# Earlier weight loads, tables inside the pipeline and a new order of steps in a fused linear-attention and soft-MoE kernel

## The chip, the cores and the metric

The kernel runs on one core of one Trainium2 chip. The metric is the device time of one execution in microseconds (us); lower is better. Three runs of the kernel before gave a median of 171.94 us.

## The reference, cut to what matters

A recurrent linear attention over S = 768 tokens for 4 batches and 8 heads of width 48 feeds a soft mixture of experts. The program computes both in one launch.

```python
for t in range(S):                       # per batch b and head h
    cur = einsum('bhd,bhe->bhde', u*k_t, v_t)
    y[:,:,t] = einsum('bhd,bhde->bhe', r_t, state + cur)
    state = w[:,:,None]*state + einsum('bhd,bhe->bhde', k_t, v_t)
x = y as (3072, 384)
logits = x @ phi                          # phi (384, 32): 8 experts x 4 slots
slot_input = softmax(logits, 0).T @ x
for e in range(8):
    slot_out[e] = relu(slot_input[e] @ w1[e]) @ w2[e]    # w1 (384,1024), w2 (1024,384)
out = softmax(logits, 1) @ slot_out
```

## The kernel before, in words

**Work units.** Heads are taken in pairs: pair m = 4b+q is heads 2q and 2q+1 of batch b, so there are 16 pairs. Each pair has two halves of 384 tokens, which gives 32 half-pairs; the main loop (L423) runs steps i = -5 to 31, and step i finishes half-pair i. The decay is applied by tables: `table(0,q)` for k and `table(1,q)` for r are a product on VectorE (L161) and an exponential on ScalarE (L163), made from `w_rep`, the vector w copied to all partitions (loaded at L95, its logarithm at L156). All eight tables are written ahead of the loop.

**Data.** `raw` has two buffers; batch b uses buffer b % 2, with a k, an r and a v part. `load_batch` issues three transfers on SyncE's queue (k and r in L103, v in L107): k and r move in 1024 runs of 1152 bytes each, v in 2048 runs of 576 bytes. Batches 0 and 1 are asked for at the start; batch 2 is asked for in the code of step 2 and batch 3 in that of step 10, each part as soon as GpSimd or ScalarE has read the old contents. In this text k(2), r(2), v(2) are the three parts of batch 2.

**One pair's way through the engines.** `scale(m,0)` and `scale(m,1)` on GpSimd multiply k and r by their tables into `kr`, which has three buffers (L201). TensorE transposes six tiles of k into bank T0 and six of r into T1 (`t_pe`, L208); ScalarE copies them out as kT and rT (L214). TensorE turns kT back into rows in bank T0 (`b_pe`, L220), and VectorE copies those out as `kn` (L225, the row copy). VectorE multiplies T1 with kT into `prod` (L230, the product). For half-pair i: `v_cast` on ScalarE turns a batch half of v into bf16 (L239, once for 8 steps' worth of two halves), `v_pe` and `v_evac` (L254, L260) lay v out, `a_pe` (L269) makes the score tiles in the one bank pair Ab, VectorE masks them (`mask_f`, L274), `m_pe` (L284 to L299) makes the states in bank Mb, VectorE reads those (`z_evac`, L309 to L315: Z0, Z and dv), `y_pe` (L325 to L338) adds up the output and `y_evac` (L345) copies it to x. `route` (L402) does the softmax part of half-batch n over four steps; in every fourth step from step 12 on it also runs `disp` (L391), which writes bank Mb, and its read on VectorE (L396, L398).

**Order.** Every engine runs its instructions in the order of the code. In a step the transposes into T0 or T1 come first, then a, the mask, the product and row copy (both in odd steps), v, y, m, Z and dv, then `route`.

**Weights.** `load_w(n)` is issued by GpSimd behind the `scale` of its step, n = 0 to 7 for w1 (L121) and 8 to 15 for w2 (L124); called w0 to w15 here. They are turned to bf16 on the way. w1 moves in 384 runs of 4 KB a load (2 KB written), w2 in 128 runs of 12 KB (6 KB written). `W_AT` says at which step how many are issued, from step 3 on. The four last w2 loads go into buffer 0 of `raw`.

**The tail.** After the loop the last softmax parts run, then for each expert 24 small matmuls whose stationary operand is a slice of w1 with every 8th column (L512, `fo:F:nF`), then 24 with contiguous slices of w2 (L527), then the output (L547 to L553).

Of the kernel before, what the change touches and what calls it, by code (L numbers as in the profile page):

```python
# [9 lines left out]
def kernel(  # L10
# [41 lines left out]
    def O(ins):  # L52
        return tc.keep_in_program_order(ins)
# [37 lines left out]

    w_rep = cst.tile([128, H * D], f32, name="w_rep")
    wu = cst.tile([8, 128], f32, name="wu")
    O(dve.memset(wu[:], 1.0))
    O(act.dma_start(out=w_rep[:], in_=w.flatten().partition_broadcast(128)))  # L95
    wu3 = wu[:].rearrange("q (e s) -> q e s", s=64)
    O(act.dma_start(out=wu3[0:4, :, 0:D], in_=w.rearrange("(q e) d -> q e d", e=2)))
    O(act.dma_start(out=wu3[4:8, :, 0:D], in_=u.rearrange("(q e) d -> q e d", e=2)))
    O(act.preload_act_table_set("natural_log_exp_and_others"))
    phi_f = cst.tile([128, nM, ES], f32, name="phi_f")  # L100

    def load_kr(which, src, b):
        O(sp.dma_start(out=raw_of(which, b).rearrange("p (h x) -> p h x", h=H),  # L103
# [6 lines left out]
    def load_batch(b):  # L110
        load_kr(0, k, b)
        load_kr(1, r, b)
        load_v(b)

    load_batch(0)
    O(sp.dma_start(out=phi_f[:], in_=moe_phi.rearrange("(mo p) s -> p mo s", p=128)))
    load_batch(1)

    def load_w(n):
        if n < E:  # L120
            O(pool.dma_start(out=w1_all[:, n, :, :],  # L121
                             in_=moe_w1[n].rearrange("(mo p) f -> p mo f", p=128)))
        else:
            O(pool.dma_start(out=w2_of(n - E),  # L124
                             in_=moe_w2[n - E].rearrange("(p fo) d -> p fo d", p=128)))


    s_i = cst.tile([128, J], i32, name="s_i")
# [38 lines left out]
    for j in range(1, NKR):
        O(dve.memset(kr_t[j][:], 0.0))
    table(0, 1)
    table(1, 1)  # L170
# [8 lines left out]
    O(pe.transpose(Yb[:, 0:8], wu[:], ident_f[0:8, 0:8]))  # L179
    wuT = cst.tile([128, 8], f32, name="wuT")  # L180
    O(dve.tensor_copy(wuT[:], Yb[:, 0:8]))
    O(dve.tensor_mul(ucol[0:64, :, 0], wuT[0:64, 0:4], wuT[0:64, 4:8]))
    O(dve.tensor_mul(ucol[64:128, :, 1], wuT[64:128, 0:4], wuT[64:128, 4:8]))
    wT = cst.tile([128, nQ], f32, name="wT")
    O(act.activation(out=wT[:], in_=wuT[:, 0:4], func=AF.Ln))
    O(act.activation(out=wT[:], in_=wT[:], func=AF.Exp, scale=float(T)))
    for q in range(2, nQ):
        table(0, q)
        table(1, q)

# [195 lines left out]
    def disp(n, first):  # L386
        x, Le = st["x", n], st["Le", n]
        for mi in range(nM + 1):
            for c in range(L):
                lhs = x[:, c, mi * C:(mi + 1) * C] if mi < nM else ones[:]  # L390
                O(pe.matmul(ds_p[:, mi * ES:(mi + 1) * ES], lhs, Le[:, c, :],  # L391
                            start=(first and mi == 0 and c == 0), stop=(c == L - 1), skip_group_check=True))

    def disp_ev(n):
        if n == 0:
            O(dve.tensor_copy(acc[:], ds_p))  # L396
        else:
            O(dve.tensor_add(acc[:], acc[:], ds_p))  # L398

    LAG = 2 * nQ  # L400

    def route(i):  # L402
        n, s = divmod(i - LAG, nQ)
        if s == 0 and 0 <= n - 1 < nG:
            disp(n - 1, False)
            disp_ev(n - 1)
            le_t(n - 1)
        if 0 <= n < nG:
            if 1 <= s <= L:
                lg_mm(n, s - 1)  # L410
            if s < L:
                xt_mm(n, s)
        if s == 0 and 0 <= n - 1 < nG:
            let_ev(n - 1)
        if 0 <= n < nG:
            if s == L:
                le_ev(n)
            if s < L:
                xt_ev(n, s)

    W_AT = {3: 1, 5: 1, 7: 1, 9: 1, 11: 1, 13: 1, 15: 1, 17: 1, 19: 1, 20: 1, 21: 1, 22: 1, 23: 4}
    nw = 0
    for i in range(-5, nH):  # L423
        m2, odd = divmod(i, 2)
        mk = m2 + 2
        if odd == 0:
            if 0 <= mk < nU:
                t_pe(mk, 0)
                t_evac(mk, 0)
        elif 0 <= mk < nU:  # L430
            t_pe(mk, 1)
            t_evac(mk, 1)
            b_pe(mk)
        if odd == 1:
            if 0 <= m2 + 3 < nU:
                scale(m2 + 3, 0)
        elif 0 <= m2 + 2 < nU:
            scale(m2 + 2, 1)
        if i % 8 == 4 or i % 8 == 5:
# [3 lines left out]
        if 0 <= i + 1 < nH:
            a_pe(i + 1)
            mask_f(i + 1)
        if odd == 1 and 0 <= mk < nU:
            prod_f(mk)
            b_evac(mk)
        if 0 <= i + 2 < nH:
            v_pe(i + 2)  # L450
            v_evac(i + 2)
        if 0 <= i < nH:
            y_pe(i)
            y_evac(i)
        if 0 <= i + 1 < nH:
            m_pe(i + 1)
            z_evac(i + 1)
# [126 lines left out]
```

## Time and profile before

| | |
|---|---|
| median of 3 runs (lowest, highest) | 171.94 us (171.04, 172.51) |
| profiled execution, whole time | 171.09 us |
| its span in the profile | 169.3 us |
| busy TensorE, VectorE, ScalarE, GpSimd | 66%, 63%, 51%, 35% of the span |
| granted TensorE clock, mean of the span | 0.872 |

A profile row gives start and duration in us. A chain row is one piece of the chain of work that ended last. "L201" is a line of the kernel. In a row of instructions "[1.70 <-DMA ...]" is the idle time of the engine ahead of it and what ended it. PEclk is the granted TensorE clock in tenths, for 40 slices of 4.23 us each.

### The profile page before, as it was taken

The numbers are of one execution on the slowest core, as the hardware profiler recorded it, in microseconds if no ns is written. First come the engines' busy times: TensorE is split into PE (matmuls) and PEld (weight loads), VectorE is DVE, ScalarE is ACT, GpSimd is POOL, SyncE is SP. The second block draws the span as 40 slices with busy tenths as digits, with TensorE's granted clock in tenths as the row PEclk, the third lists the DMA queues.
The fourth block names the chain that finished last, engine by engine and source line by source line (L and its number), as shares of the span: only waits on it lengthen the run. The fifth ranks groups of instructions, "written<-read, shape, count | busy, mean of one in ns | idle before, by whom it ended". The sixth has DMA issues, their size and how long they took to land.

```text
span 169.3 us, 4612 instructions
## 1 busy us (share of the span) xinstructions
PE 112.3 (66%) x1964; PEld 94.1 (56%) x1964; DVE 105.8 (63%) x204; ACT 86.0 (51%) x173; POOL 58.5 (35%) x59
## 2 busy tenths in 40 slices
PE   0021019776877977877876886885976999986750
PEld 0011018665756866666665675674755999972310
DVE  4099921999779889589589589589463000126550
ACT  2142594554566776886576885663454111004560
POOL 5039697666537854656668300000000000000000
PEclk9999999999699999999999999999599655555555
DMA  4999999999999999999999999200000000002896
GB/s 103 288 374 285 390 305 344 326 242 218 233 275 267 283 236 239 233 237 208 210 215 213 225 208 215 49 4 0 6 0 4 0 4 0 4 4 93 348 415 258
DMA packets 22524, 32.00 MB, mean 189 GB/s; under 512 B 1000, under 2 KB 17512, under 8 KB 22504
## 3 DMA queue, kind: packets, MB, share of 16 engines
q0 software_dynamic: 4352, 12.58, 37.9%
q1 hardware_dynamic: 17984, 18.92, 34.1%
q10 hardware_dynamic: 168, 0.20, 0.7%
q8 instruction: 15, 0.25, 0.6%
q14 instruction: 5, 0.04, 0.1%
HBM read 39.57 MB, written 4.72 MB: 262 GB/s over the span
## 4 chain that ended last, share of the span: by engine, by line
PE 48%; DVE 30%; issue 8%; ACT 7%; DMA 4%; DVEq 0%; ACTq 0%
DVE AT L274 9%; PE T L208 8%; DVE kn L225 5%; PE Ab L269 5%; DVE W L161 5%; PE Vb L254 5%; DMA w_rep<-in_w_dram 4%; DVE prod L230 4%; PE Ab L512 4%; PE T L220 3%; PE Mb L391 2%; PE Ab L547 2%; PE Vb L512 2%; PE Xb L512 2%; PE Ab L527 2%
## 5 line engine op out<-in xcount | busy, mean ns | idle before, releaser
L201 POOL TENSOR_TENSOR kr<-raw,W 128x576 bf16<-128x576 f32 x32 | 45.8, 1439 | 37.2 <-PE T L208 18.7
L274 DVE TENSOR_TENSOR AT<-Ab,mask_ut 128x768 bf16<-128x768 f32 x32 | 30.6, 957 | 13.6 <-PE Ab L269 13.5
L208 PE MATMUL T<-ident,kr 128*128 128x128 bf16 x192 | 17.5, 233 | 23.4 <-DVE kn L225 18.6
L208 PEld LDWEIGHTS <-kr 128*128 128x128 bf16 x192 | 13.6, 104 | 25.2 <-issue 20.0
L214 ACT COPY kT<-T 128x768 bf16<-128x768 bf16 x16 | 12.8, 797 | 19.4 <-PE T L208 19.4
L254 PE MATMUL Vb<-v_bf,Q 128*128 128x96 bf16 x288 | 19.2, 216 | 0.0
L230 DVE TENSOR_TENSOR prod<-T,kT 128x768 bf16<-128x768 bf16 x16 | 15.2, 948 | 3.2 <-ACT rT L214 3.2
L254 PEld LDWEIGHTS <-Q 128*128 128x128 bf16 x288 | 14.4, 103 | 3.5 <-issue 0.6
L260 ACT CAST vn<-Vb 128x288 bf16<-128x288 f32 x32 | 12.7, 398 | 5.1 <-PE Vb L254 2.7
L315 DVE TENSOR_TENSOR dv<-vn,Mb 128x288 bf16<-128x288 bf16 x32 | 14.2, 445 | 0.0
L345 ACT CAST x<-Yb 128x288 bf16<-128x288 f32 x32 | 12.8, 399 | 2.3 <-PE Yb L338 2.3
L220 PE MATMUL T<-ident,kT 128*128 128x128 bf16 x96 | 9.0, 237 | 7.1 <-ACT kT L214 7.1
L214 ACT COPY rT<-T 128x768 bf16<-128x768 bf16 x16 | 12.8, 798 | 1.3 <-PE T L208 1.3
L313 DVE TENSOR_TENSOR Z<-Mb,bmask 128x192 bf16<-128x192 f32 x32 | 11.3, 352 | 2.8 <-PE Mb L299 0.9
L512 PEld LDWEIGHTS <-w_all 128*128 128x128 bf16 x192 | 11.9, 168 | 1.3 <-issue 1.2
L295 PE MATMUL Mb<-vn,kn 128*128 128x96 bf16 (+2 forms) x80 | 11.9, 250 | 0.0
L269 PE MATMUL Ab<-rT,kT 64*128 64x128 bf16 x192 | 11.4, 228 | 0.0
L220 PEld LDWEIGHTS <-kT 128*128 128x128 bf16 x96 | 6.8, 107 | 7.4 <-ACT kT L214 7.4
L325 PE MATMUL Yb<-vn,AT 128*128 128x48 bf16 x192 | 10.3, 186 | 0.1
L338 PE MATMUL Yb<-dv,ident 128*128 128x288 bf16 x32 | 9.4, 295 | 0.2
L369 ACT COPY xT<-Xb 128x384 bf16<-128x384 bf16 x18 | 8.5, 473 | 1.9 <-PE Xb L360 1.1
L336 PE MATMUL Yb<-Z,rT 128*128 128x96 bf16 x80 | 8.8, 208 | 0.7 <-DVE Z L313 0.7
(120 smaller groups left out, 215.9 us busy)
## 6 DMA issues: line engine op xcount, KB each, us to landing
w_all<-in_moe_w_dram POOLq DMA_DIRECT2D x8, 768.0 KB, 10.3
raw<-in_k_dram SPq DMA_DIRECT2D x4, 1152.0 KB, 9.1
raw<-in_r_dram SPq DMA_DIRECT2D x4, 1152.0 KB, 11.7
raw<-in_v_dram SPq DMA_DIRECT2D x4, 1152.0 KB, 19.1
w_own<-in_moe_w_dram POOLq DMA_DIRECT2D x4, 768.0 KB, 9.2
raw<-in_moe_w_dram POOLq DMA_DIRECT2D x4, 768.0 KB, 14.5
out_dram<-raw SPq DMA_DIRECT2D x3, 768.0 KB, 3.3
out_dram<-W SPq DMA_DIRECT2D x2, 768.0 KB, 3.6
```

What stands on the lines that cost most here:

```text
L201: O(pool.tensor_mul(kr[:, j].rearrange("p j (h s) -> p j h s", s=64)[:, :, :, 0:D], src, W[j][:, q].rearrange("p j (h d) -> p j h d", h=2)))
L208: O(pe.transpose(bank[:, x * C:(x + 1) * C], kr[:, j, x, :], ident[:]))
L214: O(act.copy(t[:].rearrange("p (s j) -> p s j", j=J), bank[:, 0:S].rearrange("p (j s) -> p s j", j=J)))
L220: O(pe.transpose(T0[:, c * C:(c + 1) * C], kT[:, c * C:(c + 1) * C], ident[:]))
L230: O(dve.tensor_mul(pr[:].rearrange("p (s j) -> p s j", j=J), T1[:, 0:S].rearrange("p (j s) -> p s j", j=J), st["kT", m][:].rearrange("p (s ...
L254: O(pe.matmul(Vb[:, c * P2:(c + 1) * P2], Q3[:, o:o + C], vb[:, 2 * q:2 * q + 2, j, :], start=(j == 0), stop=(j == JV - 1)))
L260: O(act.copy(vn[:].rearrange("p c e d -> p (c e d)"), Vb[:, 0:L * P2]))
L269: O(pe.matmul(Ab[:, e, c * C:(c + 1) * C], kT[s, t], rT[s, t]))
L274: O(dve.tensor_mul(AT[:], Ab[:, :, 0:T].rearrange("p e (c t) -> p e c t", c=L), mask_ut[:, None, None, :].to_broadcast([128, 2, L, C])))
L315: O(dve.tensor_mul(dv[:], st["v", i][:].rearrange("p c e d -> p (c e) d"), Mb[:, 288:288 + 2 * L, None].to_broadcast([128, L * 2, D])))
L345: O(act.copy(st["x", n][:, :, q * P2:(q + 1) * P2], Yb[:, 0:L * P2].rearrange("p (c e) -> p c e", c=L)))
L512: O(pe.matmul(hp[:, fo, :], w1_all[:, e, mi, fo:F:nF], uns[:, mi, e * Spe:(e + 1) * Spe], start=(mi == 0), stop=(mi == nM - 1)))
```

## The change

Line numbers of the changed kernel are a few lower than those of the kernel before from L94 on (L201 becomes L196, L512 becomes L507).

- **Start.** `w_rep` is the first transfer of SyncE's queue instead of the first of ScalarE's; phi comes behind batch 1. Only the padding columns of `kr` are cleared, not the whole tiles. Two small products (`ucol`) go from VectorE to GpSimd, ahead of its first `scale`.
- **Tables.** Only the tables of q = 0 are made ahead of the loop; the other six are made in steps -4 to 1, at the end of a step's code.
- **Order of a step.** a, mask, [even step: product], y, v, m, Z and dv, `scale`, TensorE's part of `route`, then the transposes into T0 or T1, [odd step: rows back and the row copy], `v_cast`, ScalarE's part of `route`, table.
- **Weights.** `W_AT` starts at step -1 instead of 3 and ends at 22 instead of 23. w1 is read in 12 KB runs (128 runs, 6 KB written, three rows of w1 to a partition), w2 in 6 KB runs (256 runs). For that, dispatch takes every third column of x, and L512 takes every 4th column of w1 instead of every 8th.

```diff
-    O(act.dma_start(out=w_rep[:], in_=w.flatten().partition_broadcast(128)))
+    O(sp.dma_start(out=w_rep[:], in_=w.flatten().partition_broadcast(128)))
...
-                             in_=moe_w1[n].rearrange("(mo p) f -> p mo f", p=128)))
+                             in_=moe_w1[n].rearrange("(p mo) f -> p mo f", p=128)))
...
-                             in_=moe_w2[n - E].rearrange("(p fo) d -> p fo d", p=128)))
+            O(pool.dma_start(out=w2_of(n - E).rearrange("p (a y) d -> p a (y d)", y=FB),
+                             in_=moe_w2[n - E].rearrange("(a p y) d -> p a (y d)", p=128, y=FB)))
...
-    O(dve.memset(kr_t[0][:], 0.0))
+    for t in kr_t:
+        O(dve.memset(t[:].rearrange("p a j (e s) -> p (a j e) s", s=64)[:, :, D:64], 0.0))
...
-    for q in range(2, nQ):
-        table(0, q)
-        table(1, q)
...
-                lhs = x[:, c, mi * C:(mi + 1) * C] if mi < nM else ones[:]
+                lhs = x[:, c, mi:Dm:nM] if mi < nM else ones[:]
...
-    W_AT = {3: 1, 5: 1, 7: 1, 9: 1, 11: 1, 13: 1, 15: 1, 17: 1, 19: 1, 20: 1, 21: 1, 22: 1, 23: 4}
+    W_AT = {-1: 1, 1: 1, 3: 1, 5: 1, 7: 1, 9: 1, 11: 1, 13: 1, 15: 1, 17: 1, 19: 1, 20: 1, 21: 2, 22: 2}
...
+        q, j = divmod(i + 6, 2)
+        if 1 <= q < nQ:
+            table(j, q)
...
-                O(pe.matmul(hp[:, fo, :], w1_all[:, e, mi, fo:F:nF],
+                O(pe.matmul(hp[:, fo, :], w1_all[:, e, mi, (fo // FB) * C * FB + fo % FB:(fo // FB + 1) * C * FB:FB],
```

GpSimd of the kernel before, from the scale of pair 3 on (kr0, kr1, kr2 are the three buffers, raw0 and raw1 the two batches, W0 and W1 the k and r tables):

```order
L201 TENSOR_TENSOR kr0_115<-raw0_67,W0_122 128x12x48
L201 TENSOR_TENSOR kr0_115<-raw0_67,W1_123 128x12x48
L201 TENSOR_TENSOR kr1_116<-raw1_68,W0_122 128x12x48
L121 DMA w1_all_69<-in_moe_w1_dram 128x3x1024
L201 TENSOR_TENSOR kr1_116<-raw1_68,W1_123 128x12x48
L201 TENSOR_TENSOR kr2_117<-raw1_68,W0_122 128x12x48
L121 DMA w1_all_69<-in_moe_w1_dram 128x3x1024
```

GpSimd of the changed kernel, from the scale of pair 2 on:

```order
L196 TENSOR_TENSOR kr2_117<-raw0_67,W0_124 128x12x48
L123 DMA w1_all_69<-in_moe_w1_dram 128x3072
L196 TENSOR_TENSOR kr2_117<-raw0_67,W1_125 128x12x48
L196 TENSOR_TENSOR kr0_115<-raw0_67,W0_124 128x12x48
L123 DMA w1_all_69<-in_moe_w1_dram 128x3072
L196 TENSOR_TENSOR kr0_115<-raw0_67,W1_125 128x12x48
L196 TENSOR_TENSOR kr1_116<-raw1_68,W0_124 128x12x48
L123 DMA w1_all_69<-in_moe_w1_dram 128x3072
```

Load w0 now follows the first scale of pair 2 instead of that of pair 4, so each load wn follows pair n+2 instead of n+4; three loads are issued before the second scale of pair 4, and two of them before batch 0's buffer is free for batch 2.

ScalarE of the changed kernel ahead of and in steps -4 and -3 (before, all eight L163 rows stood ahead of the first copy of kT):

```order
L166 ACTIVATE W0_124<-W0_124 128x576
L166 ACTIVATE W1_125<-W1_125 128x576
L184 ACTIVATE wT_143<-wuT_139 128x4
L185 ACTIVATE wT_143<-wT_143 128x4
L209 COPY kT_157<-T0_71 128x768
L234 CAST v_bf_159<-raw0_67 128x1152
L166 ACTIVATE W0_124<-W0_124 128x576
L209 COPY rT_170<-T1_72 128x768
L234 CAST v_bf_180<-raw0_67 128x1152
L166 ACTIVATE W1_125<-W1_125 128x576
```

The tables of pair 1 now stand behind the casts of v(0), one behind each.

VectorE in two steps of the loop, the kernel before (odd step, then even step):

```order
L274 TENSOR_TENSOR AT_562<-Ab_73,mask_ut_105 128x768
L230 TENSOR_TENSOR prod_564<-T1_72,kT_495 128x768
L225 COPY kn_566<-T0_71 128x768
L309 SCALAR_TENSOR_TENSOR Z0_597<-Mb_74,wT_147,bmask_134 128x96
L313 TENSOR_TENSOR Z_599<-Mb_74,bmask_134 128x192
L315 TENSOR_TENSOR dv_596<-vn_517,Mb_74 128x288
L274 TENSOR_TENSOR AT_618<-Ab_73,mask_ut_105 128x768
L313 TENSOR_TENSOR Z_648<-Mb_74,bmask_134 128x192
L315 TENSOR_TENSOR dv_647<-vn_577,Mb_74 128x288
```

And in the changed kernel (odd step, then even step):

```order
L269 TENSOR_TENSOR AT_547<-Ab_73,mask_ut_105 128x768
L304 SCALAR_TENSOR_TENSOR Z0_578<-Mb_74,wT_143,bmask_130 128x96
L308 TENSOR_TENSOR Z_580<-Mb_74,bmask_130 128x192
L310 TENSOR_TENSOR dv_577<-vn_518,Mb_74 128x288
L220 COPY kn_598<-T0_71 128x768
L269 TENSOR_TENSOR AT_609<-Ab_73,mask_ut_105 128x768
L225 TENSOR_TENSOR prod_611<-T1_72,kT_537 128x768
L308 TENSOR_TENSOR Z_641<-Mb_74,bmask_130 128x192
L310 TENSOR_TENSOR dv_640<-vn_569,Mb_74 128x288
```

The product has moved to the even step, and the row copy to the end of the odd step, behind Z and dv.

## Rows read from the trace of the kernel before

**Rows 1.** Page, part 2: granted clock and DMA share in 40 slices.

```profile
PEclk9999999999699999999999999999599655555555
DMA  4999999999999999999999999200000000002896
```

**Rows 2.** Chain that ended last, its start: start us, us, what.

```profile
15.87 5.16 DVE W L161 x4
21.06 0.68 ACT W L163
21.74 0.69 ACT kT L214
```

**Rows 3.** Timeline, start: start us, us, engine line op, tiles, count.

```profile
1.87 2.99 SPq L107 DMA_DIRECT2D raw<-in_v_dram  x1
...
13.07 4.13 POOL L201 TENSOR_TENSOR kr<-raw,W 128x576 bf16<-128x576 f32 x3 [1.70 <-DMA raw<-in_r_dram]
```

**Rows 4.** DMA issues, 0 to 14 us: KB each, median us from issue to landing.

```profile
raw<-in_v_dram SPq DMA_DIRECT2D x1, 1152.0 KB, 14.4
```

**Rows 5.** Chain in the loop: transposes that open even steps 4, 12, 14, 16.

```profile
43.17 0.50 PE T L208 x6
...
66.00 0.51 PE T L208 x6
...
73.03 0.49 PE T L208 x6
...
78.50 0.50 PE T L208 x6
```

**Rows 6.** Timeline of VectorE, step 13 into step 14.

```profile
70.69 0.96 DVE L274 TENSOR_TENSOR AT<-Ab,mask_ut 128x768 bf16<-128x768 f32 x1 [1.20 <-PE Ab L269]
...
72.43 0.55 DVE L225 COPY kn<-T 128x768 bf16<-128x768 bf16 x1
...
73.84 0.96 DVE L274 TENSOR_TENSOR AT<-Ab,mask_ut 128x768 bf16<-128x768 f32 x1
```

**Rows 7.** Timeline of TensorE in step 17, v to m.

```profile
83.07 0.56 PE L254 MATMUL Vb<-v_bf,Q 128*128 128x96 bf16 x9
...
84.11 0.22 PE L299 MATMUL Mb<-ucol,prod 128*128 128x2 bf16 x3
```

**Rows 8.** DMA queues, 38 to 42 us: kind, packets, MB, share of 16 engines.

```profile
q0 software_dynamic: 337, 0.69, 90.3%
q1 hardware_dynamic: 334, 0.19, 21.9%
```

**Rows 9.** DMA queues, 82 to 86 us.

```profile
q0 software_dynamic: 157, 0.86, 104.6%
```

**Rows 10.** DMA queues, 27 to 31 us.

```profile
q1 hardware_dynamic: 1374, 1.56, 108.4%
```

**Rows 11.** DMA queues, 22 to 24 us.

```profile
q1 hardware_dynamic: 1229, 0.71, 112.8%
```

**Rows 12.** Timeline of SyncE and GpSimd: issue of k(2), of the first weight load.

```profile
23.67 0.37 SPq L103 DMA_DIRECT2D raw<-in_k_dram  x1
...
27.97 0.94 POOL L121 DMA_DIRECT2D w_all<-in_moe_w_dram  x1
```

**Rows 13.** Timeline of ScalarE, step 12: first cast of batch 2's v.

```profile
67.23 1.16 ACT L239 CAST v_bf<-raw 128x1152 bf16<-128x1152 f32 x1
```

**Rows 14.** Line L512: duration ns min/median/max, first and last start.

```profile
L512 PEld LDWEIGHTS <-w_all x192: 142/168/174, 130.5 to 143.4; 128*128 128x128 bf16 x192
```

**Rows 15.** Line L527, the same.

```profile
L527 PEld LDWEIGHTS <-raw x96: 103/104/105, 148.4 to 151.3; 128*128 128x128 bf16 x96
```

**Rows 16.** Chain in the tail.

```profile
131.22 1.56 PE Vb L512 x24
...
143.66 1.73 PE Mb L517 x24
...
148.51 0.64 PE Vb L527 x24
```

More of the change, by code (lines that the diff above doesn't have):

```diff
@@ L73, in w2_of @@
         return t.rearrange("p (f d) -> p f d", f=nF)
+    FB = 4
     def raw_of(which, b):
@@ L93 @@
     wu = cst.tile([8, 128], f32, name="wu")
+    wu3 = wu[:].rearrange("q (e s) -> q e s", s=64)
+    phi_f = cst.tile([128, nM, ES], f32, name="phi_f")
+    O(act.preload_act_table_set("natural_log_exp_and_others"))
+    O(sp.dma_start(out=w_rep[:], in_=w.flatten().partition_broadcast(128)))
     O(dve.memset(wu[:], 1.0))
-    O(act.dma_start(out=w_rep[:], in_=w.flatten().partition_broadcast(128)))
-    wu3 = wu[:].rearrange("q (e s) -> q e s", s=64)
     O(act.dma_start(out=wu3[0:4, :, 0:D], in_=w.rearrange("(q e) d -> q e d", e=2)))
     O(act.dma_start(out=wu3[4:8, :, 0:D], in_=u.rearrange("(q e) d -> q e d", e=2)))
-    O(act.preload_act_table_set("natural_log_exp_and_others"))
-    phi_f = cst.tile([128, nM, ES], f32, name="phi_f")
     def load_kr(which, src, b):
@@ L115 @@
     load_batch(0)
+    load_batch(1)
     O(sp.dma_start(out=phi_f[:], in_=moe_phi.rearrange("(mo p) s -> p mo s", p=128)))
-    load_batch(1)
     def load_w(n):
@@ L121, in load_w @@
             O(pool.dma_start(out=w1_all[:, n, :, :],
-                             in_=moe_w1[n].rearrange("(mo p) f -> p mo f", p=128)))
+                             in_=moe_w1[n].rearrange("(p mo) f -> p mo f", p=128)))
         else:
-            O(pool.dma_start(out=w2_of(n - E),
-                             in_=moe_w2[n - E].rearrange("(p fo) d -> p fo d", p=128)))
+            O(pool.dma_start(out=w2_of(n - E).rearrange("p (a y) d -> p a (y d)", y=FB),
+                             in_=moe_w2[n - E].rearrange("(a p y) d -> p a (y d)", p=128, y=FB)))
     s_i = cst.tile([128, J], i32, name="s_i")
@@ L166 @@
     table(1, 0)
[L167 to L170, printed above, removed]
     bmask = cst.tile([128, P2], f32, name="bmask")
@@ L181 @@
     O(dve.tensor_copy(wuT[:], Yb[:, 0:8]))
-    O(dve.tensor_mul(ucol[0:64, :, 0], wuT[0:64, 0:4], wuT[0:64, 4:8]))
-    O(dve.tensor_mul(ucol[64:128, :, 1], wuT[64:128, 0:4], wuT[64:128, 4:8]))
+    O(pool.tensor_mul(ucol[0:64, :, 0], wuT[0:64, 0:4], wuT[0:64, 4:8]))
+    O(pool.tensor_mul(ucol[64:128, :, 1], wuT[64:128, 0:4], wuT[64:128, 4:8]))
     wT = cst.tile([128, nQ], f32, name="wT")
@@ L400, with route @@
     LAG = 2 * nQ
-    def route(i):
+    def route(i, part):
         n, s = divmod(i - LAG, nQ)
[L404 to L412, printed above, removed]
+        if part == 0:
+            if s == 0 and 0 <= n - 1 < nG:
+                disp(n - 1, False)
+                disp_ev(n - 1)
+                le_t(n - 1)
+            if 0 <= n < nG:
+                if 1 <= s <= L:
+                    lg_mm(n, s - 1)
+                if s < L:
+                    xt_mm(n, s)
+            return
         if s == 0 and 0 <= n - 1 < nG:
@@ L419, in route @@
                 xt_ev(n, s)
-    W_AT = {3: 1, 5: 1, 7: 1, 9: 1, 11: 1, 13: 1, 15: 1, 17: 1, 19: 1, 20: 1, 21: 1, 22: 1, 23: 4}
+    W_AT = {-1: 1, 1: 1, 3: 1, 5: 1, 7: 1, 9: 1, 11: 1, 13: 1, 15: 1, 17: 1, 19: 1, 20: 1, 21: 2, 22: 2}
     nw = 0
     for i in range(-5, nH):
[L424 to L439, printed above, removed]
+        mu, odd = divmod(i, 2)
+        if 0 <= i + 1 < nH:
+            a_pe(i + 1)
+            mask_f(i + 1)
+        if odd == 0 and 0 <= mu + 1 < nU:
+            prod_f(mu + 1)
+        if 0 <= i < nH:
+            y_pe(i)
+            y_evac(i)
+        if 0 <= i + 2 < nH:
+            v_pe(i + 2)
+            v_evac(i + 2)
+        if 0 <= i + 1 < nH:
+            m_pe(i + 1)
+            z_evac(i + 1)
+        if odd and 0 <= mu + 3 < nU:
+            scale(mu + 3, 0)
+        if not odd and 0 <= mu + 2 < nU:
+            scale(mu + 2, 1)
+        route(i, 0)
+        if 0 <= mu + 2 < nU:
+            t_pe(mu + 2, odd)
+            t_evac(mu + 2, odd)
+            if odd:
+                b_pe(mu + 2)
+                b_evac(mu + 2)
+        if i % 8 in (4, 5):
             n = (i + 4) // 8 * 2 + (i % 8 - 4)
@@ L442 @@
                 v_cast(n)
[L443 to L457, printed above, removed]
+        route(i, 1)
+        q, j = divmod(i + 6, 2)
+        if 1 <= q < nQ:
+            table(j, q)
         if i == 2:
             O(dve.tensor_copy(phi_s[:], phi_f[:]))
-        route(i)
-        if i == 2:
             load_batch(2)
```

## The prediction

> **What bounds the kernel now.** I read the slices first, then the chain, then the waits of one step, then the DMA queues. [...] The chain [rows 2] shows the start: the first copy of kT waits until 21.74, because all eight tables stand ahead of it; the last four of them hold the chain for 5.16 us. In the loop [rows 5] a pair of steps without dispatch takes 5.47 us (73.03 to 78.50) and one with dispatch 7.03 (66.00 to 73.03). VectorE's part of that [rows 6] is a mask and a product of 0.87 each (1.74 from the mask at 70.69 to the copy at 72.43) and 1.41 for row copy, Z0, Z and dv. In the tail [rows 16] the w1 matmuls hold the chain from 131.22 to 143.66, 12.4 us, about 1.5 us for 24, while the same number with w2 takes 0.64.
>
> **Which transfers are served.** This decides the forecast. While a weight load and a raw load are both under way, 337 weight runs and 334 raw runs move in the same 4 us [rows 8]: one run for one run, whatever their length. Alone, 1374 runs of k or r move in 4 us [rows 10], 343 per us, and 1229 of v in 2 us [rows 11], 615 per us. So k or r needs 3.0 us alone and v 3.3. The weight runs of 12 KB move at 157 in 4 us alone [rows 9], 128 of them (one changed w1 load) in 3.3 us; I take 3.7 with the raw runs that slip in between and the seam between two loads. In the changed kernel a raw load beside a weight load therefore gets 128 runs per 3.7 us, against 128 x 3 in about 4.6 us before (384 runs at 337 in 4 us).
>
> **The start.** v(0) is issued at 1.87 and lands 14.4 later, at 16.3 [rows 3, 4]; with w first in the same queue I take 15.5. ScalarE then does in order: cast 1.16 [rows 13], table 0.68 [rows 2], rT 0.7, cast 1.16, table 0.68: the tables of pair 1 are ready at 17.4 and 19.9, those of pair 2, one copy of vn and one of kT or rT later each, at 21.7 and about 24.5, those of pair 3 at 28 and 31. GpSimd's scale (4.13 for three, 1.4 each [rows 3]) follows each. Six tables in the loop also cost VectorE time, 0.7 to 1.3 each (5.16 for four in [rows 2]), which is in these times. The cleared padding, the phi move and the two small products on GpSimd stand ahead of the second scale, which waits for r until 13 us now [rows 3]; that wait hides them, so I cost them at nothing; without it the products would cost a scale's time, 1.4, at most each. Step 4 then starts its mask at 36.8, against 43.98 now (0.8 after the transposes at 43.17): 7 us gained.
>
> **The loop, without transfers.** VectorE's order becomes mask, product, Z, dv and mask, Z0, Z, dv, row copy. In the odd step y, v and m need 1.26 us of TensorE after dv (83.07 to 84.33 [rows 7]), the mask fills 0.87 of it, so 0.4 is idle: 0.87 + 0.4 + 0.86 + 0.5 = 2.6. The even step is 0.87 + 0.87 + 0.27 + 0.45 = 2.45. Sum 5.1 for 5.47. A dispatch pair does not gain: disp still waits for dv, and the next a now stands behind disp, the turns and the transposes, 1.7 us after dv (1.20 idle now [rows 6]); and ScalarE's copy of the turned x comes after kT. I take 7.2 for 7.03, and 8.3 where a cast of v (1.16) stands ahead of that copy. Steps 4 to 12 take 4 x 5.1 = 20.4 against 22.8 (43.17 to 66.00). Step 12 would want its cast of v(2) at 59.7; now it starts at 67.23 [rows 13].
>
> **The weights take the engines.** Now w0 is issued at 27.97, behind k(2) at 23.67 [rows 12], so batch 2 comes first. In the changed kernel w0 is issued at 23.1 (scale of pair 2), k(2) at 29.5 (scale of pair 3), w1 at 29.5, and then one load per two scales and one issue (2 x 1.4 + 0.9 = 3.7, the issue by [rows 12]): w2 34.1, w3 37.8, w4 41.5, w5 45.2. No packet of w0 moved until after 31 in [rows 10], 3 us after its issue; a third of the runs should start in a third of that, 1.0 to 1.4; I take 1.3. So w1 moves 30.8 to 34.5 and w2 to w5 without a gap 35.4 to 50.2. k(2) gets 5 x 128 runs beside them and 0.9 us alone (309): it lands at 50.3. That releases the scale of pair 8 (with 0.5 for the wait, 50.8 to 52.2) and behind it w6, 53.5 to 57.2; r(2) lands at 53.3. The next two scales release w7 at 56.6. v(2) by then has 0.2 us alone (123), 128 beside w6 and 0.7 us alone (430); w7, w8, w9 follow without a gap until 69.0 and give it 3 x 128. The last 983 runs take 1.6 us: it lands at 70.6, usable at 71.1, 11 us after step 12 wants it. w10 cannot be issued meanwhile: it stands behind scales that wait for TensorE, which waits for ScalarE.
>
> **The sum.** Cast until 72.3, two copies until 73.2, 1.7 us of TensorE at the low clock (after such a wait I expect it, as in the dip to 0.6 at 42 us in [rows 1]), row copy: the mask of step 14 at 75.4 against 73.84 [rows 6], 1.6 late, 2.3 with 0.7 for the clock. From there: four plain pairs -0.37 each, two dispatch pairs +0.2, one +1.3, together +0.2. Batch 3 follows with the engines to itself (9.3 us, until 80), before w10 starts at 81 to 82, and step 20 wants it near 96.
> Tail: the stationary loads of w1 take 168 ns each at every 8th column and 104 for a contiguous w2 slice [rows 14, 15]; the pace is 61 and 27 ns (1.46 and 0.64 us for 24 [rows 16]). Every 4th column lies between: a gain of 0 to 8 x (1.55 - 0.65) = 7.2. I take 6.5, near the contiguous row, because the step is halved and the slow row is the far end of the only two that there are. Dispatch's step of 3 is nearer still to the contiguous row; it costs at most 9 x 34 ns, 0.3 us a dispatch, 2.4 us if all eight pay it, and I leave it at nothing.
> 171.09 (profiled execution) + 2.3 + 0.2 - 6.5 = 167.1. The median of the three runs stands 0.85 above that execution; I forecast **167**.
>
> [...]
>
> **The rivals.**
> 1. *Raw loads are not held up.* If the engines serve several raw runs for one long weight run, or v(2) slips in ahead of w7 and v(3) ahead of w10, the cast runs at 59.7 and the clock stays: 167.1 - 11.4 - 0.7 = 155. For it: full DMA slices are no proof that the order hurts; about 600 more runs at 57 us would do. Against it: [rows 8]. Chance 0.17.
> 2. *Every 4th column is as slow as every 8th* (the side that is not faster). One mechanism, at L512: stationary loads of 160 ns or more. Then the tail gains nothing and the stall of step 12 is all that is left: 173.6. It decides as soon as less than 2.5 us of the 7.2 is gained. For it: only 104 and 168 ns are known. Chance 0.20.
> 3. *Batch 3 is starved too.* w10 to w15 are issued almost together. If k(3) lands while pair 9's transposes are already done, w10 follows it by 4 us, and v(3), with some 600 runs in, gets 256 per load of 3.9 us: 22 us more. Or each load more ahead of v(2) costs 3.7. With one of the two, 167.1 + 4 to 8: about 173. Against it: w10 waits for step 14 in my count. Chance 0.13.
>
> **How the numbers follow.** The forecast has 0.50, its own range is 164 to 171. A measurement of this kernel can tell about 1% from no change, that is 170.2 to 173.7 for the same. Of the forecast's 0.50 I put 0.45 faster, 0.03 same, 0.02 slower; of rival 1 all 0.17 faster; of rival 2 0.02, 0.08, 0.10; of rival 3 0.01, 0.04, 0.08. Sum 0.65, 0.15, 0.20. The range 157 to 176 leaves out most of rival 1 (0.12) and the end of rival 3 (0.04).
>
> **What would show it.** The start: the first copy of kT near 10 us, the mask of step 4 near 37. The transfers: in a window of 38 to 42 us about as many weight packets as raw packets, both near 140; v(2) from issue to landing near 38 us; ScalarE's fourth group of casts near 71 us with TensorE idle ahead of it, and a clock dip there. The tail: stationary loads of L507 near 104 ns, 24 in 0.65 us. The forecast is wrong if raw packets outnumber the weight packets two to one, if the cast of step 12 starts before 62 us, or if L507 keeps 1.5 us for 24.

## The result, and the profile after

The changed kernel takes 166.1 us (median of four, 164.5 to 170.5) against 171.9: two of its four executions were disturbed, and the ratio, which is made from the other two (164.5 and 164.7), is 0.958 of the time before, interval 0.951 to 0.965. The forecast was 167, with 157 to 176. The profiled execution takes 164.48 us, its span is 162.7 against 169.3. So 6.6 us are gained; this is where they come from, by the same marks as in the prediction.

| mark (us) | before | after | forecast for after |
|---|---|---|---|
| mask of step 4 starts | 43.98 | 35.94 | 36.8 |
| mask of step 12 starts | 66.81 | 55.37 | |
| cast of v(2) starts | 67.23 | 65.53 | 71.1 |
| mask of step 14 starts | 73.84 | 69.93 | 75.4 |
| reciprocal that opens the tail (csr) | 130.52 | 128.95 | |
| eight w1 groups, first start to end | 131.22 to 143.66 | 129.65 to 137.02 | 5.9 instead of 12.4 |

At step 12 the changed kernel is 11.4 us ahead of the one before. At step 14 it is 3.9 ahead, at the tail 1.6. What is left at the end is mainly the tail's own gain, 12.4 - 7.4 = 5.0 us. The loop loses what the start had won, in two pieces: 7.5 us between steps 12 and 14, and 2.3 us after that.

The page of the kernel after, part 2 (granted clock, DMA share), as [rows 1]:

```profile
PEclk9999999999999998589599699879959755555555
DMA  4999999599999999999999999950000000002996
```

The kernel before has two dips of the clock ahead of the tail, in the slices at 42 us (0.50 in 44 to 46 us) and at 119 (0.51 in 119 to 122). The changed one has one from about 63 us on (0.50 in 64 to 68), and then one every 13 to 14 us (0.50 in 78 to 80, 92 to 94, 105 to 107 and 119 to 121).

**The first piece.** The timeline of the kernel after: GpSimd (start us, us, engine, line, operation, tiles; in brackets how long it sat idle and on whom), with L123 as the weight loads and L196 as the scales.

```profile
22.85 0.73 POOL L123 DMA_DIRECT2D w_all<-in_moe_w_dram  x1
...
40.38 0.59 POOL L123 DMA_DIRECT2D w_all<-in_moe_w_dram  x1
...
43.73 0.59 POOL L123 DMA_DIRECT2D w_all<-in_moe_w_dram  x1
...
49.47 1.41 POOL L196 TENSOR_TENSOR kr<-raw,W 128x576 bf16<-128x576 f32 x1 [3.71 <-DMA raw<-in_k_dram]
50.83 0.59 POOL L123 DMA_DIRECT2D w_all<-in_moe_w_dram  x1
61.85 1.39 POOL L196 TENSOR_TENSOR kr<-raw,W 128x576 bf16<-128x576 f32 x1 [10.43 <-DMA raw<-in_r_dram]
...
64.56 0.59 POOL L123 DMA_DIRECT2D w_all<-in_moe_w_dram  x1
```

Its DMA queues, 39 to 43 us (q0 the weights, q1 the raw loads; packets, MB, share of 16 engines), which answer to [rows 8]:

```profile
q0 software_dynamic: 142, 0.78, 94.3%
q1 hardware_dynamic: 138, 0.16, 13.6%
```

ScalarE, TensorE and VectorE at the stall:

```profile
59.54 0.96 DVE L269 TENSOR_TENSOR AT<-Ab,mask_ut 128x768 bf16<-128x768 f32 x1 [0.87 <-PE Ab L264]
...
65.53 1.15 ACT L234 CAST v_bf<-raw 128x1152 bf16<-128x1152 f32 x1 [5.47 <-DMA raw<-in_v_dram]
...
67.48 0.26 PE L348 MATMUL Xb<-phi_s,xT 128*128 128x32 bf16 x3 [6.79 <-ACT xT L364]
...
69.93 0.95 DVE L269 TENSOR_TENSOR AT<-Ab,mask_ut 128x768 bf16<-128x768 f32 x1
```

Read from the bottom: TensorE sits 6.8 us because ScalarE has not copied the turned x; that copy stands behind the cast of v(2); the cast waits until 65.5 for v(2). GpSimd waits 3.7 us for k(2) and 10.4 for r(2). And in the queues one raw run moves for each weight run of up to 12 KB, 138 beside 142 in 4 us. From the mask at 59.54 to the one at 69.93 are 10.4 us, where the same step of the next dispatch pair takes 3.1 (79.73 to 82.87).

**The second piece.** From step 14 to the last mask the kernel before takes 73.84 to 122.91, the one after 69.93 to 121.20: 49.1 and 51.3. Pairs without dispatch fall from 5.47 to 4.82 (one takes 4.98), pairs with dispatch rise from 7.03 to 8.1 to 8.6. A dispatch pair in the timeline of the kernel after:

```profile
77.24 0.42 PE L386 MATMUL Mb<-Lexp,x 128*128 128x32 bf16 x9 [1.71 <-DVE dv L310]
...
79.29 0.80 ACT L209 COPY kT<-T 128x768 bf16<-128x768 bf16 x1 [3.54 <-PE T L203]
...
79.73 0.96 DVE L269 TENSOR_TENSOR AT<-Ab,mask_ut 128x768 bf16<-128x768 f32 x1 [1.66 <-PE Ab L264]
```

TensorE idles 1.7 us for dv, and behind that gap ScalarE waits 3.5 us for the transposes of k and VectorE 1.7 for a. The granted clock was 1.00 in 72 to 76 us; the low clock in what follows is the 0.50 of the first stretch below. The granted clock of the two stretches of the kernel after that hold the stall and this dispatch (stretch, length, busy time of each engine, clock, DMA share, GB/s):

```profile
64.00:68.00 4.00, 0.52 (x8) 0.52 (x9) 0.00 (x0) 2.46 (x5) 3.98 (x5) 0.50 1.08 386
76.00:80.00 4.00, 2.76 (x39) 2.13 (x39) 1.75 (x5) 0.71 (x2) 0.00 (x0) 0.66 1.07 221
```

**The tail.** Stationary loads of w1 and the first and last steps of that chain after (as [rows 14, 16]); the last number of a loads row before the idle time is the mean in ns:

```profile
L507 PEld LDWEIGHTS <-w_all 128*128 128x128 bf16 x192 | 6.7, 118 | 1.1 <-issue 1.1
```

```profile
129.65 0.93 PE Vb L507 x24
130.58 0.81 PE Ab L507 x24
...
137.02 1.77 PE Mb L512 x24
```

118 ns instead of 168, and 0.80 to 0.94 us for 24 instead of 1.44 to 1.56.

### The profile page after: what moved, and what is told of

It is laid out like the page before. It is cut to its first block, busy times and chain, and to the rows that moved or that the text cites. A ratio compares the mean times of both kernels' runs of the same rounds, so it can differ in the third digit from the quotient of the medians.

```text
span 162.7 us, 4640 instructions
## 1 busy us (share of the span) xinstructions
PE 112.8 (69%) x1964; PEld 92.7 (57%) x1964; DVE 97.9 (60%) x202; ACT 85.0 (52%) x173; POOL 57.7 (35%) x61
## 5 line engine op out<-in xcount | busy, mean ns | idle before, releaser
L196 POOL TENSOR_TENSOR kr<-raw,W 128x576 bf16<-128x576 f32 x32 | 44.6, 1409 | 34.3 <-DMA raw<-in_r_dram 11.6
L203 PE MATMUL T<-ident,kr 128*128 128x128 bf16 x192 | 18.6, 242 | 5.7 <-POOL kr L196 5.7
L249 PEld LDWEIGHTS <-Q 128*128 128x128 bf16 x288 | 17.7, 106 | 5.4 <-issue 4.2
L220 DVE COPY kn<-T 128x768 bf16<-128x768 bf16 x16 | 8.9, 554 | 14.7 <-PE T L215 14.5
L234 ACT CAST v_bf<-raw 128x1152 bf16<-128x1152 f32 x8 | 9.2, 1154 | 8.3 <-DMA raw<-in_v_dram 8.3
L331 PE MATMUL Yb<-Z,rT 128*128 128x96 bf16 x80 | 10.5, 217 | 2.7 <-DVE Z L308 2.7
L320 PE MATMUL Yb<-vn,AT 128*128 128x48 bf16 x192 | 10.9, 191 | 0.0
L333 PE MATMUL Yb<-dv,ident 128*128 128x288 bf16 x32 | 10.0, 311 | 1.3
L386 PE MATMUL Mb<-Lexp,x 128*128 128x32 bf16 x72 | 3.3, 180 | 9.5 <-DVE dv L310 8.6
L320 PEld LDWEIGHTS <-AT 128*128 128x128 bf16 x192 | 7.4, 100 | 3.7 <-issue 1.0
## 6 DMA issues: line engine op xcount, KB each, us to landing
raw<-in_v_dram SPq DMA_DIRECT2D x4, 1152.0 KB, 19.9
```

The source lines that it names most:

```text
L249: O(pe.matmul(Vb[:, c * P2:(c + 1) * P2], Q3[:, o:o + C], vb[:, 2 * q:2 * q + 2, j, :], start=(j == 0), stop=(j == JV - 1)))
L320: O(pe.matmul(Yb[:, o:o + D], AT[:, e, c, :], vn[:, c, e, :], start=first, stop=False, skip_group_check=True))
```

## The experiments

All are compared with the kernel before on the same chip. The ratios:

| kernel | us (median) | ratio to before, interval |
|---|---|---|
| changed kernel | 166.1 | 0.958, 0.951 to 0.965 |
| before + weight layout only | 165.2 | 0.966, 0.961 to 0.971 |
| before + weight layout + start | 177.7 | 1.037, 1.030 to 1.043 |
| changed, w1 in 4 KB runs | 176.9 | 1.036, 1.032 to 1.041 |
| changed, weight steps of before | 171.5 | 1.006, 1.002 to 1.009 |
| changed, weights held during 2 to 5 | 172.4 | 1.007, 1.003 to 1.011 |
| changed, raw loads first | 157.7 | 0.922, 0.915 to 0.929 |
| changed, turns ahead of dispatch | 159.6 | 0.933, 0.926 to 0.940 |
| changed, raw first and turns ahead | 150.6 | 0.880, 0.875 to 0.885 |
| the same with every 2nd column | 151.3 | 0.883, 0.876 to 0.891 |

**The layout alone.** The kernel before with `FB = 4`, the new views of w1, w2, the w1 slice and the dispatch slice.

> The kernel before with the new weight layout alone: w1 in runs of 12 KB and w2 in runs of 6 KB, every 4th column in the w1 matmuls, every 3rd in dispatch; start, step order and steps of the weight loads as before. Theory A: the tail gains what it gained in the changed kernel, 12.4 - 7.4 = 5.0 us, and the loop keeps its time, because batch 2 is issued before w0 and the weight loads come one per 5.5 us: 171.9 - 5.0 = 167 us. Theory L (the long runs starve the raw loads wherever they stand): a stall at step 12 of 3 us or more, 170 us or more.

165.2 us, ratio 0.966: 5.4 us gained by the medians, 5.8 by the ratio. (On this chip the kernel before takes 170.6 us, so theory A's 167 would be 165.6.) Its chain in the tail:

```profile
129.90 0.36 DVE csr L503
130.60 0.94 PE Vb L514 x24
...
137.97 1.75 PE Mb L519 x24
```

7.4 us for the eight groups, and csr at 129.90 instead of 130.52. Theory A: the layout is worth 5.1 us in the tail and costs the loop nothing in the order of before. Since the intervals of this kernel and of the changed one overlap, the rest of the change (start, step order, weight steps) brings, all together, nothing that these runs can tell.

**Which weight loads hold batch 2 back.** First I only moved the weight loads, in two ways.

```diff
-    W_AT = {-1: 1, 1: 1, 3: 1, 5: 1, 7: 1, 9: 1, ...
+    W_AT = {-3: 1, -1: 1, 5: 1, 6: 1, 7: 1, 8: 1, 14: 1, ... 23: 1}
```

> The changed kernel with another table of weight loads only: w0 and w1 behind the scales of steps -3 and -1, w2 to w5 in steps 5 to 8, the other ten one per step from step 14, so that no weight load is started while batch 2 (issued in step 2) or batch 3 (issued in step 10) is on its way. Theory A, the loads of batch 2 lose their turns to the weight runs, and that makes the one long stall of the changed loop (TensorE idle from 60.7 to 67.5 us, the scale that waited for r(2) started at 61.85, the cast of v(2) at 65.53): the cast of step 12 starts near 60, no wait over 2 us for raw, the low clock after the stall (63.6 to 70.5) goes: 164.5 - 6.8 - 0.7 = 157 us. Theory B, it is the volume: 16 weight loads and 12 raw loads keep the engines full whatever the order, so the wait only moves (to v(1) or v(3)): 164 us or more.

```diff
-    W_AT = {-1: 1, 1: 1, 3: 1, 5: 1, 7: 1, 9: 1, ...
+    W_AT = {3: 1, 5: 1, 7: 1, ... 19: 1, 20: 1, 21: 1, 22: 1, 23: 4}
```

> The changed kernel with the weight loads in the steps in which the kernel before has them (3, 5, 7, ... 19, 20, 21, 22, then four in step 23), nothing else changed. Theory A (one run for one run while both are under way): batch 2 has the engines to itself from 30.6 to about 35 us, k(2) and r(2) land there, and v(2) gets 128 runs beside each load and the 1 us between two loads, some 680 runs per 5 us: it lands near 51, before step 12 wants it at 59.7; batch 3 follows likewise by about 75. No stall at step 12: 157 to 158 us, as with the held table. Theory B (volume): the sixteen loads end later, the stall stays: 164 us or more.

172.4 and 171.5 us: both numbers of theory A are wrong, and by the times alone theory B would stand. The traces say otherwise. With the weight steps of before, the queues from 43 to 47 us, then GpSimd, then ScalarE:

```profile
q0 software_dynamic: 142, 0.77, 93.6%
q1 hardware_dynamic: 142, 0.08, 9.2%
```

```profile
33.70 0.73 POOL L123 DMA_DIRECT2D w_all<-in_moe_w_dram  x1
34.45 2.78 POOL L196 TENSOR_TENSOR kr<-raw,W 128x576 bf16<-128x576 f32 x2
37.18 0.60 POOL L123 DMA_DIRECT2D w_all<-in_moe_w_dram  x1
...
72.95 1.15 ACT L234 CAST v_bf<-raw 128x1152 bf16<-128x1152 f32 x1 [12.66 <-DMA raw<-in_v_dram]
```

One run for one run is exact, 142 and 142. What I had wrong was the pace of the weight loads: not one per pair of steps (5 us), but one per two scales and an issue, 3.34 us, less than the 4 us that a load takes (0.77 MB in 4 us, a load has 0.79). So from about 38 us on there is always a weight load under way, and the 2048 runs of v(2) get 36 per us. In the kernel before the same table gives 27.97, 33.38, 38.60, 45.17: there GpSimd has filled its three buffers before the loop begins, and each further scale waits for transposes. In the changed kernel it is late with its scales, since the tables are, and runs free for seven loads. The same holds for the held table: w2 was issued at 36.17, v(2) had just begun to move, and the four loads and those from 52.30 on kept its last runs until 74.1. A weight load that GpSimd has in step 5 of its program is not issued when the loop is in step 5.

**Is it the length of the run?**

```diff
-  in_=moe_w1[n].rearrange("(p mo) f -> p mo f", p=128)
+  in_=moe_w1[n].rearrange("(mo p) f -> p mo f", p=128)
-  lhs = x[:, c, mi:Dm:nM] if mi < nM else ones[:]
+  lhs = x[:, c, mi * C:(mi + 1) * C] if mi < nM else ones[:]
```

> The changed kernel with w1 read in runs of 4 KB again, three per partition (and dispatch reading contiguous columns again, which belongs to it); the weight matmuls keep every 4th column, the weight loads keep their steps. Theory L, the 12 KB run is what starves batch 2: three times as many raw runs get a turn beside each load, k(2) and r(2) land 8 to 15 us earlier and the stall at step 12 is gone: 157 us. Theory Q, it is the number of weight loads queued ahead of v(2): k(2) and r(2) land early, but then nothing holds w7 back either, w0 to w7 go through without a gap at 4.6 us each until about 61, and v(2) with 83 runs per us needs 25 us after about 41: it lands near 65, the stall stays within 2 us of what it is: 163 to 166 us. The tail keeps its 7.4 us for w1 by both.

176.9 us, slower than with 12 KB. Queues from 63 to 67 us, and the cast:

```profile
q0 software_dynamic: 344, 0.68, 89.5%
q1 hardware_dynamic: 342, 0.20, 22.3%
```

```profile
78.16 1.15 ACT L234 CAST v_bf<-raw 128x1152 bf16<-128x1152 f32 x1 [18.08 <-DMA raw<-in_v_dram]
```

Raw runs get 86 per us instead of 36, as theory L has it, and v(2) comes 12.6 us later all the same. Theory Q named the reason and undersized it: k(2) and r(2) land early, so nothing stops GpSimd, w8 and w9 are issued at 59.71 and 63.19 too, and v(2) has weight runs beside it to the end. In the changed kernel GpSimd stood for 10.4 us at the scale that waited for r(2); w7 could not start, and v(2) went through alone. The rate went with the length of the weight runs, 86 raw runs per us beside 4 KB and 36 beside 12 KB; at this table the number of weight loads beside v(2) counted for more.

**The start alone.** To the layout kernel the new start is added: w first, padding only, ucol on GpSimd, six tables at the end of the loop's steps.

> The kernel before with the new weight layout and the new start (w first on SP's queue, only the padding of kr cleared, ucol on GpSimd, the tables of pairs 1 to 3 inside the pipeline, batch 1 ahead of phi), the step order and the steps of the weight loads as before. Theory A: step 4 starts its mask near 37 instead of 43.7, and as the step order of before holds GpSimd's scales back by the transposes, the weight loads come one per 5.4 us, raw runs get the engines alone for a third of the time, and v(2) lands near 51 to 55, before step 12 wants it at 59: the whole gain of the start stays, 165.2 - 6.7 = 158.5 us. Theory E (a start that is 7 us earlier always meets its inputs later): the stall at step 12 comes here too, and 163 us or more are left.

177.7 us: the number is far on theory E's side, but the start did not come 7 us earlier, so the reason that theory E gives was not put to the test. GpSimd and the cast:

```profile
29.14 1.40 POOL L196 TENSOR_TENSOR kr<-raw,W 128x576 bf16<-128x576 f32 x1 [5.10 <-ACT W L166]
...
39.91 0.73 POOL L123 DMA_DIRECT2D w_all<-in_moe_w_dram  x1
...
43.38 0.60 POOL L123 DMA_DIRECT2D w_all<-in_moe_w_dram  x1
...
78.93 1.15 ACT L234 CAST v_bf<-raw 128x1152 bf16<-128x1152 f32 x1 [14.13 <-DMA raw<-in_v_dram]
```

The mask of step 4 starts at 42.97, only 0.8 us earlier than with the layout alone (43.73): in the old step order the tables are waited for. And the late scales again let GpSimd run free, a load each 3.4 us from 39.91 on, just when v(2) moves. The starvation thus needs neither the new step order nor the new table of weight steps nor a loop that starts much earlier.

**Raw loads first.** Now the weights are kept out until batches 2 and 3 are in.

```diff
-    W_AT = {-1: 1, 1: 1, 3: 1, 5: 1, 7: 1, 9: 1, ...
+    W_AT = {-1: 1, 14: 1, 15: 1, 16: 1, 17: 1, 18: 1, 19: 2, 20: 2, 21: 2, 22: 2, 23: 2}
```

> The changed kernel with another table of weight loads only: w0 stays at step -1, the other fifteen are issued in steps 14 to 23, which GpSimd reaches near 52 us by the run with the held table (52.30), so that batch 2 (issued near 30) and batch 3 (issue allowed near 44) have the engines to themselves. Theory A, one run for one run between v and whatever weight load is under way: in the held table v(2) had moved for two microseconds when w2 came at 39.5 and then got only 36 runs per us until 71; without w2 to w5 in front it needs 2048/615 = 3.3 us and lands near 41, the scales and the cast of step 12 near 60 wait for nothing, the low clock after the stall goes: 157 us, 155 to 159. The weights then need 15 loads of 3.8 us, until about 112, still ahead of the tail near 121. Theory B (volume: the wait only moves): the stall moves to step 20 or to the tail, which then waits for w1 or w2: 164 us or more.

157.7 us where 157 was expected. Its queues from 37 to 41 us, the first weight load behind them, and VectorE's masks of steps 12 to 14:

```profile
q1 hardware_dynamic: 2184, 1.37, 107.6%
```

```profile
51.12 0.60 POOL L123 DMA_DIRECT2D w_all<-in_moe_w_dram  x1
...
55.36 0.95 DVE L269 TENSOR_TENSOR AT<-Ab,mask_ut 128x768 bf16<-128x768 f32 x1
...
60.33 0.96 DVE L269 TENSOR_TENSOR AT<-Ab,mask_ut 128x768 bf16<-128x768 f32 x1 [1.65 <-PE Ab L264]
64.20 0.95 DVE L269 TENSOR_TENSOR AT<-Ab,mask_ut 128x768 bf16<-128x768 f32 x1
```

2184 raw runs in 4 us without a weight run; 3.9 us from mask to mask where it was 10.4; the tail waits for no weight. Theory B falls: the volume was never the bound, the order was. This settles the first piece.

**The gap ahead of dispatch.** The six lines of transposes and copies of k and r are put ahead of `route(i, 0)`, with and without the table above.

```diff
-        route(i, 0)
         if 0 <= mu + 2 < nU:
             t_pe(mu + 2, odd)
...
+        route(i, 0)
         if i % 8 in (4, 5):
```

> The kernel of the run with batches 2 and 3 ahead of the weights, and in each step the transposes of k and r and their copies written ahead of dispatch and the transposes of x. In the changed kernel TensorE waits 1.7 to 1.8 us for dv ahead of each dispatch (five such waits, 9.0 us together) and the granted clock falls to 0.5 or 0.6 behind it. Theory G: the six transposes (0.5 us) fill part of the gap, kT is copied 0.9 us sooner, the clock stays up at some of the dispatches: 0.5 to 0.9 us for each of the seven dispatches in the loop, 3 to 6 us less than the run without this edit. Theory N: the chain of a dispatch pair runs dv, dispatch, copy of the turned x, and the transposes only change places: within 1 us of it.

> The changed kernel with only the order within a step edited: the transposes of k and r and their copies ahead of dispatch and the transposes of x; the weight loads in the steps of the changed kernel. If the two losses are apart (the stall of step 12 from the weights, the gaps ahead of dispatch from the order), this edit is worth here what it was worth with the raw loads first, 157.65 - 150.64 = 7.0 us less the one dispatch that stands in the stall anyway: 164.6 (fast runs of the changed kernel) - 6 = 158 to 159 us, with the stall of 6 to 7 us ahead of step 13's mask still there. If the gaps and the stall were one loss (a loop that runs faster meets v(2) and batch 3 later), nothing comes out: 163 us or more.

150.6 us with the raw loads first: 7.0 less, more than theory G's 3 to 6, though the loop has five dispatches and not the seven that I counted there. A dispatch pair of that kernel, and its clock from 78.5 to 82.5:

```profile
79.66 0.80 ACT L209 COPY kT<-T 128x768 bf16<-128x768 bf16 x1 [0.17 <-PE T L203]
...
80.99 0.41 PE L386 MATMUL Mb<-Lexp,x 128*128 128x32 bf16 x9 [1.36 <-DVE dv L310]
...
82.33 0.96 DVE L269 TENSOR_TENSOR AT<-Ab,mask_ut 128x768 bf16<-128x768 f32 x1 [0.54 <-PE Ab L264]
```

```profile
78.50:82.50 4.00, 2.63 (x56) 2.12 (x54) 2.88 (x7) 3.09 (x6) 1.72 (x2) 1.00 1.06 209
```

kT is copied before dispatch instead of behind it, its wait falls from 3.5 us to 0.2, and the clock stays up here, at 1.00. The pair takes 6.35 us (mask at 78.50 to mask at 84.85) where the same pair takes 8.6 with the old order. Two other pairs of the same kernel, where the clock fell all the same (0.70 in 68 to 72 us at the earlier one), take 7.8 for 8.2 and 8.3. But the first of these holds a cast of v and the two others do not, so this alone does not give the price of the clock. The last run of the next section, with the same order of steps, does: there the clock falls at a pair with a cast and stays up at one without. VectorE's masks there:

```profile
55.19 0.95 DVE L269 TENSOR_TENSOR AT<-Ab,mask_ut 128x768 bf16<-128x768 f32 x1
...
62.94 0.96 DVE L269 TENSOR_TENSOR AT<-Ab,mask_ut 128x768 bf16<-128x768 f32 x1
...
67.77 0.94 DVE L269 TENSOR_TENSOR AT<-Ab,mask_ut 128x768 bf16<-128x768 f32 x1
...
74.12 0.95 DVE L269 TENSOR_TENSOR AT<-Ab,mask_ut 128x768 bf16<-128x768 f32 x1
```

7.75 us with the low clock, 6.35 without: with a cast or without one a pair takes the same, and the low clock costs it 1.4 us. At the low clock the new order saves 0.4 to 0.5 us in a pair without a cast and 0.9 to 1.1 in one with a cast (8.84 and 8.60 with the old order). So of the 7.0 us some 2.8 are the clock that stays up at two pairs, and more than half of the rest is the order itself.

Alone, without the new table, the edit gives 159.6 us where 158 to 159 was expected. By the ratios the table is worth 3.6%, the order 2.5% (4.2 us, where I had counted on 6), and both together 7.7%, more than the sum. So neither loss is the other one in disguise, and each edit is worth somewhat more beside the other.

**The step between columns.**

```diff
-    FB = 4
+    FB = 2
```

> The changed kernel with every 2nd column in the w1 matmuls instead of every 4th (and so w2 in runs of 3 KB instead of 6 KB). One look, for the stationary loads of w1: 104 ns for contiguous columns, 118 at every 4th, 168 at every 8th. If the price comes with the distance from the first step on, every 2nd column lies between 104 and 118, near 109. If every 2nd is free and every 4th is not, it is 104. The pace of 24 matmuls is 0.64 contiguous, 0.80 at every 4th. The loop's time is not read from this run, since the shorter w2 runs change the turns as well.

> The fastest kernel so far (raw loads first, transposes ahead of dispatch) with every 2nd column in the w1 matmuls and so w2 in runs of 3 KB. Every 2nd column loaded in 104 ns like contiguous ones, every 4th in 118. If the tail pays by the load, 8 x (0.85 - 0.65) = 1.5 us come off: 149.1 us. Against it: 512 runs of 3 KB for each w2 load instead of 256 of 6 KB take the engines longer; if a w2 load takes 1 us more or so, the last one ends 8 us later, near 120, and w2 is wanted near 125, so still no wait; a wait at the second stage of the tail would show up as 151 us or more.

The stationary loads of w1 at every 2nd column:

```profile
L507 PEld LDWEIGHTS <-w_all 128*128 128x128 bf16 x192 | 5.4, 104 | 1.2 <-issue 1.2
```

104 ns, the same as contiguous. (That is a single execution; its 170.6 us are compared with nothing.) In the fastest kernel the eight groups fall to 6.1 us (117.67 to 123.78 in the chain), 1.3 less, yet the time is 151.3 against 150.6, the intervals overlap: csr came at 116.97 instead of 115.83. The clock rows of the page, with every 4th column and then with every 2nd:

```profile
PEclk9999999999999999998799999599999655555555
```

```profile
PEclk9999999999999999699999699999879655555555
```

Ahead of the tail the clock is low in two stretches of the loop with every 4th column (from 67 us and from 93) and in three with every 2nd (from 60, 82 and 105). Of the 1.1 us, 0.4 to 0.5 are there from the mask of step 4 (35.91 instead of 35.44, ahead of any dip) to that of step 28 (102.67 instead of 102.29); the other 0.8 come behind it, where the third stretch lies. Whether the shorter w2 runs have to do with it, no run here tells.

## Why the prediction was right, and where it was not

The sum came within 2.6 us of the profiled execution, for a reason that is half the predicted one, and in part by luck: errors of 6.2 us one way met errors of 3.5 us the other way. Step by step:

**The start held.** The exponentials of the six tables start at 16.86, 19.17, 20.73, 24.27, 27.30 and 30.17 and take 0.68 to 0.70 each, so they end within 0.5 us of the forecast (17.4, 19.9, 21.7, 24.5, 28 and 31), w0 and w1 go out at 22.85 and 29.46 (23.1, 29.5), and the mask of step 4 starts at 35.94 (36.8). The first copy of kT is at 12.18, not near 10; it cost nothing that shows, since the tables come when they were to.

**The plain pairs were better, the dispatch pairs worse.** 4.82 for 5.1: the wait in the odd step is 0.2, not 0.4. The dispatch pairs, forecast at 7.2, and 8.3 with a cast, take 8.1 to 8.6. The step that failed is "the next a now stands behind disp, the turns and the transposes": I counted that work at a granted clock of 1.00. Behind the gap of 1.71 us at 77.24 it was 0.66 in 76 to 80 us, and such a fall cost a pair about 1.4 us (7.75 against 6.35 above). For the stall I had written such a dip, for the dispatches not. Price: +2.2 us from step 14 to the last mask, where the loop's share of my sum was +0.2.

**One run for one run held** (142 to 138, 142 to 142, 344 to 342), and not in the counts alone: of the 64 weight runs that start between 39 and 41 us in the trace of the kernel after, 62 start 0.06 us behind the start of a raw run. Equal counts alone could also come from equal turns of several runs on both sides; the order of the single runs speaks against that. With one run for one run, rival 1 (raw loads not held up) falls: the cast was late, not at 59.7.

**The chain of releases failed in one link.** I had 3.7 us for a weight load; 0.78 MB in 4 us [the queues at 39 to 43 us] makes it 4.0, and between 43 and 55 us, with 0.70 to 0.76 MB in 4 us, it is 4.1 to 4.5. k(2) still came as forecast (its scale at 49.47; 50.8). But I let r(2) go alone from 50.2, and there was no gap: w5 and w6 followed on, r(2) landed near 61 instead of 53.3. That held GpSimd for 10.4 us, so w7, forecast at 56.6, went out at 64.56, and v(2), which was to share the engines with w7, w8 and w9, had them alone. It landed at 65, not 70.6. An error of 8 us in r(2) thus brought the cast 5.6 us forward, which nothing in my count had foreseen. The run with 4 KB is the other side of this: there r(2) is early, GpSimd does not stop, and the stall is a long one of the kind that I had forecast.

**Batch 3** was to have the engines to itself until 80. It had not: w7 to w10 follow at 64.56 to 74.91, and GpSimd waits 9.7 us ahead of the scale at 85.41, which is that of r(3): the last runs of r(3) move at 84.7. (The timeline puts that wait down to a matmul.) This is rival 3's mechanism, but it cost nothing: with raw loads first the same dispatch pairs take 8.2 to 8.6 as well.

**The tail.** 24 matmuls take 0.80 to 0.94, not 0.65. The gain is 12.4 - 7.4 = 5.0 us, the term was 6.5, its bounds 0 to 7.2. The value 118 ns lies between the two rows that I had, nearer the contiguous one, as argued; I put it too close. Rival 2 falls. The measured 118 at every 4th column against 104 at every 2nd and contiguous says that every 4th is not quite free. Dispatch at every 3rd column cost next to nothing, as taken: its loads take 104 ns, and 96 with contiguous columns in the run with 4 KB, so 9 x 8 ns or 0.07 us a dispatch.

Sum: 167.1, less 5.5 for step 14 (3.9 early instead of 1.6 late), plus 2.0 for the loop, less 0.7 for the clock that I had put in front, plus 1.5 for the tail: 164.4, against 164.48.

## What to carry to other kernels

In these runs a long transfer that nobody wanted yet cost most where it shared the engines with a short one that was wanted: 36 raw runs per us moved beside weight runs of 12 KB (142 in 4 us), 546 without them (2184 in 4 us). So count the runs that wait and the loads that can be issued in front of them, by the pace of the engine that issues them when nothing holds it back, not by the pace of the loop. A start that leaves that engine behind with its other work lets it run free later, so the table of loads has to be set anew with the start. And before work of an idle engine is reordered, look at what fills the wait ahead of the longest step: here a few transposes moved into a gap of 1.7 us were worth 4 to 7 us (2.5% to 4.1%).

## What the runs showed of the hardware

- The DMA engines took one run of the weights' queue and one of the raw queue in turn, with w1 in runs of 12 KB (142 to 142 beside v, and in the changed kernel 62 of 64 weight runs start 0.06 us behind the start of a raw run) as with 4 KB (344 to 342).
- In the changed kernel the issue of v(2) on SyncE takes 13.0 us and that of k(3), behind it, 15.8, while with raw loads first v(2)'s takes 0.53:

```profile
32.88 12.95 SPq L109 DMA_DIRECT2D raw<-in_v_dram  x1
45.92 15.77 SPq L105 DMA_DIRECT2D raw<-in_k_dram  x1
```

- In the changed kernel the granted clock of TensorE fell from 1.00 to 0.50 behind four of the five idle gaps of 1.71 us ahead of dispatch in the loop (0.50 in 78 to 80 us, 92 to 94, 105 to 107 and 119 to 121; not at 57.87 us, where it is 1.00 from 56 to 60). With the turns ahead it fell behind one gap of 1.36 us (0.70 in 68 to 72) and not behind another (1.00 in 80 to 84). Such a fall cost a dispatch pair 1.4 us (7.75 against 6.35).
- The stationary load of 128 columns takes 104 ns contiguous, 104 at every 2nd, 118 at every 4th and 168 at every 8th in the tail; in dispatch 96 contiguous and 104 at every 3rd.
